# The square between half copies at batch turns, and the passage from attention to the experts with two experts' rows turned together and w1 split one expert ahead

## The chip, the cores and the metric

One core of a Trainium2 chip runs the whole program in one launch. The metric is device time in microseconds (us), the median of several executions. The engines are TensorE (PE, matrix products), ScalarE (ACT), VectorE (DVE), GpSimd (POOL) and SyncE (SP), which issues most DMAs. TensorE's clock has two levels, 2.4 and 1.2 GHz; the profile gives the granted clock as a share of the higher one.

## The reference, cut to what matters

Eight batches of 2496 tokens go through an attention without softmax (z has 64 columns, v and u 256), and the 19968 rows that come out go through a mixture of experts: the gate picks one of eight experts a row, and each expert keeps the 80 rows with the highest gate weight.

```python
scores = scale * np.matmul(z, z.transpose(0, 2, 1))     # scale = 1 / 2496
attn = np.maximum(scores, 0.0) ** 2
x = u * np.matmul(attn, v)
...
logits = x @ w_gate                                     # 8 experts
expert_idx = np.argmax(logits, axis=1)
gate_w = softmax(logits)[row, expert_idx]
...
h = np.maximum(x[tok_idx] @ w1[e], 0.0)                 # w1[e] 256 x 1024, 80 rows
out[tok_idx] = gate_w[tok_idx, None] * (h @ w2[e])      # w2[e] 1024 x 256
```

Rows that no expert keeps stay zero.

## The kernel before, in words

Attention goes batch by batch (`b`), in five chunks of 512 queries (`qc`, the last has 448), and for each chunk over ten pairs of key tiles (`r` counts them). Two accumulators in PSUM (`acc`, one for each half `c` of the 256 columns) collect a chunk; there are two such buffers in all, so the next chunk's first product into one waits until it has been emptied. The scores `s` have one buffer. They are made two steps ahead of their use: PE writes `s`, ACT takes the relu into `a` and squares it there, ACT casts a high part `ah` and DVE subtracts the low part `al`; three products of high and low parts with the split `vt` give the precision of fp32. Scores below the diagonal are not computed again but read back transposed (`blk`); `mirrored` makes `ah` and `al` of them.

At a chunk's last pair `take` copies both accumulators to SBUF (`xf`) on ACT; `chunk_add`, `chunk_x`, `chunk_rest` and `chunk_lo` on DVE make the attention's rows from them, `chunk_logits` and `chunk_sum` the gate's logits. The gate's weights, the ranks of rows within an expert (`blocks`, `count`) and the look-ups of the rows that are likely to be kept (`lookup`, `lookup_rest`, `fetch_two`, `place_two`, `tokens`) stand between the pairs at positions that `two_at` and `finished` write out. A turn from one batch to the next is the step `r` = 9 of chunk 4.

The order on PE, ACT, DVE and POOL is the order in which the code is written (`manual_schedule`); each engine runs its own list and waits at semaphores for the others.

The passage follows the last chunk of batch 7. It finishes the last rows (`chunk_x_last`), their logits and gate, and runs the first products of experts 0 and 1 (`first_products`), with weights that were loaded and split beside the last attention chunks (`LOADS`, `SPLITS`, `kept`). Then `ahead` runs the experts: 512 KB pieces of weights come into five slots, ACT casts their high part and DVE subtracts the low part (`split`), and for each expert PE transposes its rows (`ffn_x`), takes the first product (`ffn1`), transposes the hidden rows (`ffn_h`) and takes the second (`ffn2`); `result` scales by the gate and scatters. The five slots lie where attention had its raw `z`, `v` and weights.

Of the kernel before, what the change touches and what calls it, by code (L numbers as in the profile page):

```python
# [19 lines left out]
P = 128  # L20
# [5 lines left out]
def attn_moe_kernel(ctx, tc, zT, uT, v, wg, w1, w2, out, seq, cap):  # L26
# [51 lines left out]
    zpool = main.enter_context(tc.tile_pool(name="zpool", bufs=2))  # L78
    upool = main.enter_context(tc.tile_pool(name="upool", bufs=1))
# [174 lines left out]
    two_b = [const.tile([P, DC * NS], F32, tag=f"two{i}", name=f"two{i}") for i in range(2)]  # L254
# [121 lines left out]
    def mirrored(b, qc, k):  # L376
# [15 lines left out]
    def scores(b, qc, k, later=False):

        if k // QT < qc:
            return lambda: mirrored(b, qc, k)
# [17 lines left out]
        if later:  # L413
            return lambda: (square(), split(b, qc, k, a, diag, lower, c0, nq))
        square()
        return lambda: split(b, qc, k, a, diag, lower, c0, nq)

    def split(b, qc, k, a, diag, lower, c0, nq):
# [13 lines left out]
        if diag and not lower:  # L432
            quarter_out(b, qc, a)
# [81 lines left out]
    def take(b, qc, c):  # L515
# [4 lines left out]
        nc.scalar.copy(out=x[:, :, c], in_=acc_t[b, qc][c][:, :, :x.shape[-1]])  # L520

    def chunk_add(b, qc):
        x = x_sum[b, qc]
        tt(x[:, 0], x[:, 0], x[:, 1], ALU.add)
# [14 lines left out]
    def chunk_x_last(b, qc, c):  # L539
        x, acc = x_sum[b, qc], acc_t[b, qc][c]  # L540
        for s in (slice(0, 2 * P), slice(2 * P, min(CH, seq - qc * CH))):
            nc.scalar.copy(out=x[:, 1, c, s], in_=acc[:, 1, s])
            tt(x[:, 0, c, s], acc[:, 0, s], x[:, 1, c, s], ALU.add)
            V.scalar_tensor_tensor(out=x[:, 0, c, s], in0=x[:, 0, c, s], scalar=CSQ,
                                   in1=u_t[b, qc][:, c, s], op0=ALU.mult, op1=ALU.mult)

    def chunk_logits_last(b, qc):
# [3 lines left out]
        pl = ps_m.tile([P, 2, CH], F32, tag="m", name=f"pl_{b}_{qc}")[:, 0]  # L551
# [34 lines left out]
    def raw_tile(name):  # L586
        return zpool.tile([P, DC, CH], F32, tag="vraw", name=name, bufs=3)
# [126 lines left out]
    def count(b, k0, n, slot):  # L714

        kr = RB[b] * BPB + k0
        pool, tag = (ps_a, "acc") if b == B - 1 else (ps_m, "m")
        tp = pool.tile([P, 2, CH], F32, tag=tag, name=f"tp_{b}_{k0}")[:, :, :n * E]
# [97 lines left out]
    def first_x():  # L816
        xf = xall[0][:, 0]
        xp = ps_m.tile([P, 2, CH], F32, tag="m", name="xp_first")[:, 0]
        for c in range(DC):
            nc.tensor.transpose(out=xp[:, c * NS:(c + 1) * NS], in_=xf[:NS, c * P:(c + 1) * P],  # L820
                                identity=ident[:NS, :NS])
        x_t[0] = [const.tile([P, DC * NS], F32R, tag=f"two{i}", name=f"x_first{i}") for i in range(2)]
        xh, xl = x_t[0]
        nc.scalar.copy(out=xh, in_=xp[:, :DC * NS])
        tt(xl, xp[:, :DC * NS], xh, ALU.subtract)

    h_first = {}
    x_second = [const.tile([P, DC * NS], F32R, name=f"x_second{i}") for i in range(2)]

    def first_products():  # L830
        one = vpool.tile([P, QT * 2 * D], F32, tag="vt", name="h_first")
        xp = ps_m.tile([P, 2, CH], F32, tag="m", name="xp_second")[:, 0]
        for c in range(DC):
            nc.tensor.transpose(out=xp[:, c * NS:(c + 1) * NS], in_=xall[0][:NS, 1, c * P:(c + 1) * P],
                                identity=ident[:NS, :NS])
        x_t[1] = x_second
        nc.scalar.copy(out=x_t[1][0], in_=xp[:, :DC * NS])
        tt(x_t[1][1], xp[:, :DC * NS], x_t[1][0], ALU.subtract)
        hp = ps_s.tile([P, 2, CH], F32, tag="s", name="hp_first")
        for part in range(2):  # L840
            product1(hp[:, part], 0, 0, part, NS)
        h_first[0] = one[:, :F]
        nc.scalar.activation(out=h_first[0][:NS], in_=hp[:NS].rearrange("p a f -> p (a f)"), func=AF.Relu)
        hp = ps_a.tile([P, 2, CH], F32, tag="acc", name="hp_second")
        for part in range(2):
            product1(hp[:, part], 1, 1, part, NS)
        h_first[1] = vpool.tile([P, QT * 2 * D], F32, tag="vt", name="h_second")[:, :F]
        nc.scalar.activation(out=h_first[1][:NS], in_=hp[:NS].rearrange("p a f -> p (a f)"), func=AF.Relu)
# [13 lines left out]
    def both(f, *es):  # L862
        for e in es:
            f(e)

    two_at = {(2, 2, 3): lookup, (2, 2, 4): lookup_rest,
              (2, 2, 5): lambda: both(fetch_two, 0, 1),
              (2, 2, 9): lambda: (both(place_two, 0, 1), both(fetch_two, 2, 3)),
              (2, 3, 7): lambda: (both(place_two, 2, 3), both(fetch_two, 4, 5)),
              (3, 2, 3): lambda: (both(place_two, 4, 5), both(fetch_two, 6, 7)),  # L870
              (3, 3, 8): lambda: both(place_two, 6, 7),
              (4, 2, 3): tokens,
              (4, 2, 4): lambda: fetch_gates(range(4)), (4, 2, 5): lambda: fetch_gates(range(4, E))}
# [44 lines left out]
    def load_raw(e, which, part, after=None):  # L918
        pool, tag, n = (late["raw"], "wraw", None) if "raw" in late else (zpool, "vraw", 3)
# [69 lines left out]
    SPLITS = dict(zip([(qb, 2), (qb, 4), (qb, 6), (qb, 7), (qz, 2), (qz, 6), (qz, 8), (qz, 9)], early))  # L989
# [21 lines left out]
    def weights_ahead(qc, r):  # L1011
# [11 lines left out]
        if qc == NQ - 1 and r >= NP - 2:  # L1023
            split_hi(*kept[r - NP + 2][0], kept[r - NP + 2][1])
# [21 lines left out]
    def finished(b, qc, r):  # L1046
# [589 lines left out]
```

## Time and profile before

| what | us |
|---|---|
| median of 3 runs | 1327.08 |
| lowest and highest | 1325.53, 1327.59 |
| the profiled execution | 1328.22 |
| its span, first to last instruction | 1326.5 |
| PE, DVE, ACT busy in it | 1300.0, 1063.0, 1017.0 |

The span leaves out the start and the end of the launch, 1.7 us here. The chain of work that ended last runs through PE for 76% of the span. Busy shares are means over stages: attention takes the first 1254 us, the passage some 20, the experts the rest. The mean granted clock of TensorE is 0.994.

### The profile page before, as it was taken

The numbers are of one execution on the slowest core, as the hardware profiler recorded it, in microseconds if no ns is written. First come the engines' busy times: TensorE is split into PE (matmuls) and PEld (weight loads), VectorE is DVE, ScalarE is ACT, GpSimd is POOL, SyncE is SP. The second block draws the span as 40 slices with busy tenths as digits, with TensorE's granted clock in tenths as the row PEclk, the third lists the DMA queues.
The fourth block names the chain that finished last, engine by engine and source line by source line (L and its number), as shares of the span: only waits on it lengthen the run. The fifth ranks groups of instructions, "written<-read, shape, count | busy, mean of one in ns | idle before, by whom it ended". The sixth has DMA issues, their size and how long they took to land.

```text
span 1326.5 us, 31268 instructions
## 1 busy us (share of the span) xinstructions
PE 1300.0 (98%) x13119; PEld 1074.3 (81%) x13119; DVE 1063.0 (80%) x1276; ACT 1017.0 (77%) x1102; POOL 42.8 (3%) x58
## 2 busy tenths in 40 slices
PE   9999999999999999999999999999999999999997
PEld 6888877888877888888888888888888888887786
DVE  8878788678888888787987788877887879867785
ACT  8976688767878688776887778886887768878665
POOL 0000000000001000000003000000000000002011
PEclk9999999999999999999999999999999999999989
DMA  7799768894898949998699958999499985789473
GB/s 215 247 292 265 221 197 242 246 275 158 260 283 248 277 138 280 270 280 244 175 289 280 288 171 236 285 277 269 149 289 277 275 245 161 235 237 269 146 255 119
DMA packets 196132, 317.21 MB, mean 239 GB/s; under 512 B 36192, under 2 KB 119056, under 8 KB 185744
## 3 DMA queue, kind: packets, MB, share of 16 engines
q1 hardware_dynamic: 194704, 312.85, 79.7%
q0 software_dynamic: 1280, 2.30, 0.6%
q8 instruction: 104, 1.70, 0.5%
q14 instruction: 44, 0.36, 0.1%
HBM read 168.77 MB, written 141.21 MB: 234 GB/s over the span
## 4 chain that ended last, share of the span: by engine, by line
PE 76%; DMA 8%; ACT 6%; DVE 4%; issue 3%; SPq 2%; POOL 0%; POOLq 0%; DVEq 0%; ACTq 0%
PE acc L449 61%; PE s L407 10%; DMA blk<-y 3%; DMA y<-x 3%; DVE al L58 2%; ACT a L409 2%; PE pl L612 2%; ACT a L411 1%; PE op L1393 1%; ACT xf L520 1%; PE hp L858 1%; SPq L343 1%; ACT ah L387 1%; DMA zraw<-zT 1%; DMA vraw<-v 1%
## 5 line engine op out<-in xcount | busy, mean ns | idle before, releaser
L449 PE MATMUL acc<-ah,vt 64*128 64x512 f32 (+1 forms) x6240 | 954.4, 383 | 1.3 <-ACT xf L520 1.0
L449 PEld LDWEIGHTS acc<-ah,vt 64*128 64x128 f32 x6240 | 586.6, 184 | 115.6 <-ACT xf L520 8.9
L449 PE MATMUL acc<-al,vt 64*128 64x512 f32 (+1 forms) x3120 | 612.3, 383 | 4.5 <-DVE al L58 4.0
L58 DVE TENSOR_TENSOR al<-a,ah 128x1024 fp32r<-128x1024 f32 (+1 forms) x240 | 270.7, 1128 | 151.1 <-ACT ah L114 147.7
L449 PEld LDWEIGHTS acc<-al,vt 64*128 64x128 f32 x3120 | 300.2, 184 | 66.8 <-DVE al L58 13.0
L409 ACT ACTIVATE a<-s 128x1024 f32<-128x1024 f32 x240 | 229.0, 954 | 148.7 <-PE s L407 127.5
L411 ACT ACTIVATE a<-a 128x1024 f32<-128x1024 f32 x240 | 238.0, 992 | 7.4
L58 DVE TENSOR_TENSOR al<-blk,ah 128x1024 fp32r<-128x1024 f32 x160 | 192.6, 1218 | 51.4 <-ACT ah L387 49.5
L387 ACT CAST ah<-blk 128x1024 fp32r<-128x1024 f32 x160 | 163.9, 1050 | 83.2 <-PE acc L449 75.7
L114 ACT CAST ah<-a 128x1024 fp32r<-128x1024 f32 (+3 forms) x217 | 213.5, 984 | 5.9
L316 DVE STREAM_TRANSPOSE x<-a 128x1024 f32<-128x1024 f32 x160 | 198.1, 1238 | 0.0
L58 DVE TENSOR_TENSOR xf<-xf 128x1024 f32<-128x1024 f32 (+3 forms) x117 | 144.5, 1235 | 0.0
L520 ACT COPY xf<-acc 128x1024 f32<-128x1024 f32 (+1 forms) x78 | 76.8, 996 | 22.5 <-PE acc L449 21.3
L407 PE MATMUL s<-zl,zh 64*128 64x512 f32 x480 | 89.7, 370 | 0.0
L407 PE MATMUL s<-zh,zl 64*128 64x512 f32 x480 | 89.7, 370 | 0.0
L407 PE MATMUL s<-zh,zh 64*128 64x512 f32 x320 | 64.1, 397 | 3.7 <-ACT a L409 3.7
L407 PEld LDWEIGHTS s<-zl,zh 64*128 64x128 f32 x480 | 45.1, 184 | 8.3
L407 PEld LDWEIGHTS s<-zh,zl 64*128 64x128 f32 x480 | 45.2, 185 | 6.8
L147 DVE TENSOR_TENSOR vt<-vraw,vt 128x1024 fp32r<-128x1024 f32 x40 | 48.3, 1207 | 0.0
L528 DVE SCALAR_TENSOR_TENSOR xf<-xf,ut 128x1024 f32<-128x1024 f32 (+1 forms) x39 | 45.8, 1174 | 0.0
L407 PEld LDWEIGHTS s<-zh,zh 64*128 64x128 f32 x320 | 30.1, 184 | 12.2 <-ACT a L409 6.7
L58 DVE TENSOR_TENSOR al<-md,ah 128x512 fp32r<-128x512 f32 x37 | 25.1, 679 | 12.7 <-ACT ah L427 11.2
(198 smaller groups left out, 660.9 us busy)
## 6 DMA issues: line engine op xcount, KB each, us to landing
y<-x SPq DMA_DIRECT2D x80, 1024.0 KB
blk<-y SPq DMA_DIRECT2D x320, 256.0 KB
out<-idle SPq DMA_DIRECT2D x40, 512.0 KB
vraw<-v SPq DMA_DIRECT2D x32, 512.0 KB
ut<-uT SPq DMA_DIRECT2D x32, 512.0 KB
xu<-xf SPq DMA_DIRECT2D x32, 512.0 KB
wraw<-w SPq DMA_DIRECT2D x30, 512.0 KB
yd<-xd SPq DMA_DIRECT2D x37, 256.0 KB
```

What stands on the lines that cost most here:

```text
L58: V.tensor_tensor(out=o, in0=a, in1=b, op=op)
L114: eng.copy(out=o, in_=i)
L147: e1.tensor_tensor(out=vt[:, :, 1], in0=raw, in1=vt[:, :, 0], op=ALU.subtract)
L316: V.transpose(out=x[:, :, :, t:t + 2].rearrange("p n k t s -> p t k n s"), in_=a)
L387: nc.scalar.copy(out=natural(ah), in_=src)
L407: nc.tensor.matmul(s[:, h, c0:c1], zk[hs, t * P:(t + 1) * P], zq[hs], start=n == 0, stop=n == 2)
L409: nc.scalar.activation(out=a[:, :, c0:c1], in_=s[:, :, c0:c1], func=AF.Relu)
L411: nc.scalar.activation(out=a[:, :, c0:c1], in_=a[:, :, c0:c1], func=AF.Square)
L449: nc.tensor.matmul(acc_t[b, qc][c][:, h, :nq], v_t[b, k // QT][hs, k % QT, iv, c * P:(c + 1) * P], x[hs, k % 2, :nq], start=at not in begu ...
L520: nc.scalar.copy(out=x[:, :, c], in_=acc_t[b, qc][c][:, :, :x.shape[-1]])
L528: V.scalar_tensor_tensor(out=x[:, 0], in0=x[:, 0], scalar=CSQ, in1=u_t[b, qc][:, :, :x.shape[-1]], op0=ALU.mult, op1=ALU.mult)
L612: nc.tensor.matmul(to[:, h, t], xb[i % 3][hs, i // 3, t0:t0 + P], wgs[hs, i // 3], start=i == 0, stop=i == 3 * DC - 1)
```

## The change

In attention: at every chunk's last pair the square of the scores that are made ahead stands between the two accumulators' copies (`between`), where it stood before the copies, or, at batch turns, behind them. For the last chunk of a batch ACT copies only one half of an accumulator and DVE adds the other half out of PSUM. The mirrored pair made at the last pair of a chunk is cast in two halves if the next chunk is 2 or 4. The tables of blocks come a chunk later; look-ups, placings and the low parts of `v` stand at other pairs; gates are gathered one expert a pair.

In the passage: the rows of experts 0 and 1 are transposed together, ahead of the last chunk's end; both first products, expert 0's turn, its second product and its scaling stand in the passage, and the remaining splits between them. In `ahead` the loop begins with expert 1's hidden rows, the pieces of w1 come one expert ahead of w2, and the indices of rows (`rows_out`) are copied on POOL. Raw weights and `v` have a pool of their own (`rawpool`), so that the five slots of `ahead` no longer lie over them.

```diff
+    rawpool = main.enter_context(tc.tile_pool(name="rawpool", bufs=3))
...
-    def mirrored(b, qc, k):
+    def mirrored(b, qc, k, part=None):
...
+        if not part:
+            a_t[b, qc, k] = [pair_tile(tag, b, qc, k) for tag in ("ah", "al")]
+        ah, al = a_t[b, qc, k]
+        nc.scalar.copy(out=natural(ah), in_=src[:, rows])
+        tt(natural(al), src[:, rows], natural(ah), ALU.subtract)
...
         if k // QT < qc:
-            return lambda: mirrored(b, qc, k)
+            if turn and qc % 2 == 0:
+                return None, lambda: (mirrored(b, qc, k, 0), mirrored(b, qc, k, 1))
+            return None, lambda: mirrored(b, qc, k)
...
-        nc.scalar.copy(out=x[:, :, c], in_=acc_t[b, qc][c][:, :, :x.shape[-1]])
+        acc = acc_t[b, qc][c][:, :, :x.shape[-1]]
+        if qc < NQ - 1:
+            nc.scalar.copy(out=x[:, :, c], in_=acc)
+        else:
+            nc.scalar.copy(out=x[:, 1, c], in_=acc[:, 1])
+            tt(x[:, 0, c], acc[:, 0], x[:, 1, c], ALU.add)
...
-    two_at = {(2, 2, 3): lookup, (2, 2, 4): lookup_rest,
...
+    two_at = {(2, 3, 7): lookup, (2, 4, 4): lookup_rest,
...
-            elif r == 9 and b <= 2:
-                kr = RB[b - 1] * BPB
-                blocks(ps_m, "m", gp, oh, kr, kr + BPB, wtwo, (b - 1) * BPB)
+        elif qc == 1 and 0 < b <= 2 and r == 2:
+            kr = RB[b - 1] * BPB
+            blocks(ps_m, "m", gp, oh, kr, kr + BPB, wtwo, (b - 1) * BPB)
...
-                attend_pair(b, qc, 2 * p, True, True, lambda c: take(b, qc, c))
+                def between(c):
+                    take(b, qc, c)
+                    if c == 0:
+                        if square:
+                            square()
+                        while turned:
+                            turned.pop()()
+
+                attend_pair(b, qc, 2 * p, True, True, between)
...
+    def first_turns():
+        tp = first["tp"] = ps_s.tile([P, 2, CH], F32, tag="s", name="tp_first")
+        for j in range(FC):
+            to = tp[:, j * 2 // FC, j % (FC // 2) * NS:(j % (FC // 2) + 1) * NS]
+            nc.tensor.transpose(out=to, in_=h_first[0][:NS, j * P:(j + 1) * P], identity=ident[:NS, :NS])
...
+            for x, w in ((hh, w2h), (hh, w2l), (hl, w2h)):
+                nc.tensor.matmul(op[:NS], x[:, i, at], w[:, j], start=n == 0, stop=n == 3 * FC - 1)
+                n += 1
...
-        first_products()
+        first_product(0)
+        p = SPLITS.pop(None)
+        split_w(*p, w_raw.pop(p), V)
+        first_relu(0)
+        first_product(1)
+        split_rest()
         split_rest()
         gate_near(b, 0)
+        first_turns()
         chunk_store(*prev)
         chunk_logits_last(*prev)
+        first_hidden()
+        first_relu(1)
         count(b, 0, BPB - 2, b)
         gate_top(b, NQ - 1, NQ)
         gate_exp(b, NQ - 1)
+        first_second()
         gate_near(b, NQ - 1)
         gate_rows(b, ex_last, gp, nc.gpsimd)
+        first_result()
...
-            pieces = [(e, w, part) for e in range(E) for w in (1, 2) for part in range(2)
-                      if (e, w, part) not in early and (e, w) not in RAW.values()]
+            pieces = [(e, w, part) for i in range(2, E + 1) for e, w in ((i, 1), (i - 1, 2)) for part in range(2)
+                      if e < E and (e, w, part) not in early and (e, w) not in RAW.values()]
...
-                ts(slo_i[e][:NS], nh[0][1][:NS, e:e + 1], 0.0, ALU.add)
+                nc.gpsimd.tensor_scalar(out=slo_i[e][:NS], in0=nh[0][1][:NS, e:e + 1], scalar1=0.0,
+                                        scalar2=None, op0=ALU.add)
```

ScalarE at the first batch turn: `acc_4_0` and `acc_4_1` are the last chunk's accumulators, `a_0_4` and `a_0_6` scores of the next batch. Before:

```order
L409 ACTIVATE a_0_4_2456<-s_0_4_2457 128x1024
L520 COPY xf_4_2477<-acc_4_0_2092 128x2x448
L520 COPY xf_4_2477<-acc_4_1_2093 128x2x448
L411 ACTIVATE a_0_4_2456<-a_0_4_2456 128x1024
L114 CAST ah_0_4_2487<-a_0_4_2456 128x1024
L409 ACTIVATE a_0_6_2495<-s_0_6_2496 128x1024
```

Now:

```order
L415 ACTIVATE a_0_4_2457<-s_0_4_2458 128x1024
L536 COPY xf_4_2478<-acc_4_0_2097 128x448
L417 ACTIVATE a_0_4_2457<-a_0_4_2457 128x1024
L536 COPY xf_4_2478<-acc_4_1_2098 128x448
L115 CAST ah_0_4_2492<-a_0_4_2457 128x1024
L415 ACTIVATE a_0_6_2501<-s_0_6_2502 128x1024
```

The square stands between the copies, and each copy has one half of 448 elements instead of both.

VectorE at the same turn, from the first low part of the next batch on (`xd` is the transposed diagonal, `vt` a split of `v`, `lg` the sum of logits). Before:

```order
L58 TENSOR_TENSOR al_0_0_2424<-a_0_0_2413,ah_0_0_2423 128x1024
L352 STREAM_TRANSPOSE xd_0_2427<-a_0_0_2413 128x2x2x4x32
L619 TENSOR_REDUCE lg_1166<-pl_3_2358 128x32
L147 TENSOR_TENSOR vt_3_2411<-vraw_3_2085,vt_3_2411 128x4x256
L58 TENSOR_TENSOR al_0_4_2488<-a_0_4_2456,ah_0_4_2487 128x1024
L316 STREAM_TRANSPOSE x_1_0_2491<-a_0_4_2456 128x2x4x4x32
```

Now:

```order
L58 TENSOR_TENSOR al_0_0_2429<-a_0_0_2418,ah_0_0_2428 128x1024
L58 TENSOR_TENSOR xf_4_2478<-acc_4_0_2097,xf_4_2478 128x448
L353 STREAM_TRANSPOSE xd_0_2482<-a_0_0_2418 128x2x2x4x32
L58 TENSOR_TENSOR xf_4_2478<-acc_4_1_2098,xf_4_2478 128x448
L58 TENSOR_TENSOR al_0_4_2493<-a_0_4_2457,ah_0_4_2492 128x1024
L317 STREAM_TRANSPOSE x_1_0_2496<-a_0_4_2457 128x2x4x4x32
L638 TENSOR_REDUCE lg_1167<-pl_3_2363 128x32
```

Two additions out of PSUM stand around the transpose `xd`, and the split of `vt` has gone to another place.

TensorE in the passage, from the last product of attention on (`hp` first products, `pl` logits, `op` second products, `xp` and `tp` transposes of rows and hidden rows). Before:

```order
L449 MATMUL acc_4_1_17848<-ah_4_18_18134,vt_4_16024 128x448
L834 MATMUL xp_second<-ident,xall 128x112 x2
L858 MATMUL hp_first<-w1h_43_17523,x_first_17905 112x512
L858 MATMUL hp_second<-w1h_47_17937,x_second_215 112x512
L553 MATMUL pl_4_18276<-idle 128x32
L557 MATMUL pl_4_18276<-wg_sb,xf_4_18194 128x8 x8
L722 MATMUL tp_0_18286<-oh,ones_b 128x64
L1378 MATMUL tp_0_18367<-ident,h_first 128x112 x4
L1378 MATMUL tp_4_18374<-ident,h_first 128x112 x4
L1348 MATMUL xp_18381<-ident,xall 128x112 x2
L1449 MATMUL tp_end<-oh,ones_b 128x8
L1393 MATMUL op_18422<-w2h_45_17680,hTh_18365 112x256
```

Now:

```order
L461 MATMUL acc_4_1_17888<-ah_4_18_18176,vt_4_16060 128x448
L901 MATMUL hp_first_18267<-w1h_43_17561,x_first_17947 112x512
L901 MATMUL hp_first_18284<-w1h_47_17979,x_first_17947 112x512
L869 MATMUL tp_first<-ident,h_first_18282 128x112 x8
L572 MATMUL pl_4_18315<-idle 128x32
L576 MATMUL pl_4_18315<-wg_sb,xf_4_18230 128x8 x8
L743 MATMUL pl_4_18315<-oh,ones_b 128x64
L886 MATMUL op_first<-w2h_45_17718,hT_firsth 112x256
L1409 MATMUL xp_18427<-ident,xall 128x112 x2
L1436 MATMUL tp_0_18442<-ident,h_first_18331 128x112 x4
L1436 MATMUL tp_4_18449<-ident,h_first_18331 128x112 x4
```

Of each run of products the first row stands here. The transposes of expert 1's rows have gone from the head of the passage, and expert 0's turn stands ahead of the logits and its second product right behind the count, where three sets of transposes and the count of the end stood between.

## Rows read from the trace of the kernel before

**Rows 1.** The page's first part: busy time and share of the span.

```profile
PE 1300.0 (98%) x13119; PEld 1074.3 (81%) x13119; DVE 1063.0 (80%) x1276; ACT 1017.0 (77%) x1102; POOL 42.8 (3%) x58
```

**Rows 2.** Waits of PE: line, waited for, us in total, times, longest.

```profile
PE s L407 <- ACT a L409: 4.9, 8, 1.1
PE acc L449 <- DVE al L58: 4.0, 12, 0.5
...
PE wp L884 <- DVE lg L619: 1.3, 2, 0.7
PE acc L449 <- ACT xf L520: 1.0, 2, 0.8
```

**Rows 3.** Timeline at a batch turn: start, us, instruction, idle before it.

```profile
1096.69 1.73 ACT L520 COPY xf<-acc 128x896 f32<-128x896 f32 x2
1098.32 1.06 ACT L411 ACTIVATE a<-a 128x1024 f32<-128x1024 f32 x1
...
1100.36 1.02 ACT L409 ACTIVATE a<-s 128x1024 f32<-128x1024 f32 x1
...
1096.71 0.70 DVE L352 STREAM_TRANSPOSE xd<-a 128x512 f32<-128x512 f32 x1
...
1100.06 0.62 PE L449 MATMUL acc<-ah,vt 64*128 64x512 f32 x4
1100.51 0.39 PE L449 MATMUL acc<-al,vt 64*128 64x512 f32 x2
1101.43 0.50 PE L407 MATMUL s<-zh,zh 64*128 64x512 f32 x2 [0.54 <-ACT a L409]
```

**Rows 4.** Timeline at the beginning of a chunk qc=4.

```profile
1071.26 2.94 ACT L387 CAST ah<-blk 128x1024 fp32r<-128x1024 f32 x3
...
1072.35 2.36 DVE L58 TENSOR_TENSOR al<-blk,ah 128x1024 fp32r<-128x1024 f32 x2 [2.35 <-ACT ah L387]
...
1072.76 0.57 PE L449 MATMUL acc<-ah,vt 64*128 64x448 f32 x4
1073.62 0.47 PE L449 MATMUL acc<-al,vt 64*128 64x448 f32 x2 [0.30 <-DVE al L58]
```

**Rows 5.** Timeline of PE in the passage.

```profile
1253.82 0.41 PE L834 MATMUL xp_second<-ident,xall 112*128 112x112 f32 x2
...
1259.03 0.48 PE L858 MATMUL hp_second<-w1h,x_second 128*112 128x512 f32 x1 [2.03 <-ACT x_second L837]
...
1267.86 1.73 PE L1378 MATMUL tp<-ident,h_first 112*128 112x112 f32 x8 [2.33 <-DVE d_last L58]
...
1270.22 0.54 PE L1393 MATMUL op<-w2h,hTh 128*112 128x256 f32 x1
...
1274.83 0.93 PE L1378 MATMUL tp<-ident,h_second 112*128 112x112 f32 x8
```

**Rows 6.** Busy time by stretch: stretch, length, engines (instructions), PE's granted clock, DMA share, GB/s.

```profile
1264.00:1266.00 2.00, 1.52 (x15) 1.40 (x15) 0.32 (x2) 0.44 (x1) 0.00 (x0) 1.00 1.00 337
...
1268.00:1270.00 2.00, 2.00 (x13) 1.92 (x14) 1.83 (x5) 0.91 (x2) 0.00 (x0) 0.50 0.34 97
...
1280.00:1290.00 10.00, 10.00 (x75) 8.83 (x74) 8.98 (x19) 7.93 (x13) 0.96 (x1) 1.00 0.85 282
1290.00:1300.00 10.00, 10.00 (x70) 8.84 (x69) 9.07 (x15) 9.12 (x13) 1.88 (x2) 1.00 0.82 251
```

**Rows 7.** Timeline of the expert stage: SP, DVE, PE and ACT.

```profile
1256.57 2.44 SPq L925 DMA_DIRECT2D wraw<-w  x5
...
1273.57 2.36 DVE L947 TENSOR_TENSOR w1l<-wraw,w1h 128x1024 fp32r<-128x1024 f32 x2
...
1309.02 0.15 DVE L62 TENSOR_SCALAR idx<-sel 112x1 int32<-112x1 f32 x1
1309.08 1.15 DVE L58 TENSOR_TENSOR hTl<-tp,hTh 128x448 fp32r<-128x448 f32 x2
...
1311.64 0.35 PE L1393 MATMUL op<-w2h,hTh 128*112 128x256 f32 x1
...
1317.98 0.47 ACT L1400 ACTIVATE ob<-op,gates 112x256 f32<-112x256 f32 x1 [2.34 <-PE op L1393]
```

More of the change, by code (lines that the diff above doesn't have):

```diff
@@ L411, in square, with cast @@
             nc.scalar.activation(out=a[:, :, c0:c1], in_=a[:, :, c0:c1], func=AF.Square)
[L413 to L414 removed]
+        def cast():
+            split(b, qc, k, a, diag, lower, c0, nq)
+        if turn:
+            return square, cast
         square()
[L416 removed]
+        return None, cast
     def split(b, qc, k, a, diag, lower, c0, nq):
@@ L540, in chunk_x_last @@
         x, acc = x_sum[b, qc], acc_t[b, qc][c]
[L541 to L545, printed above, removed]
+        s = slice(0, min(CH, seq - qc * CH))
+        nc.scalar.copy(out=x[:, 1, c], in_=acc[:, 1, s])
+        tt(x[:, 0, c], acc[:, 0, s], x[:, 1, c], ALU.add)
+        V.scalar_tensor_tensor(out=x[:, 0, c], in0=x[:, 0, c], scalar=CSQ, in1=u_t[b, qc][:, c, s],
+                               op0=ALU.mult, op1=ALU.mult)
     def chunk_logits_last(b, qc):
@@ L716, in count @@
         kr = RB[b] * BPB + k0
-        pool, tag = (ps_a, "acc") if b == B - 1 else (ps_m, "m")
-        tp = pool.tile([P, 2, CH], F32, tag=tag, name=f"tp_{b}_{k0}")[:, :, :n * E]
+        if b == B - 1:
+            tp = first.pop("count")[:, :, :n * E]
+        else:
+            tp = ps_m.tile([P, 2, CH], F32, tag="m", name=f"tp_{b}_{k0}")[:, :, :n * E]
         rows = [slice(0, P)] if b < 2 or b == B - 1 else HALVES
@@ L816, in first_x @@
     def first_x():
[L817 to L839, printed above, removed]
-        for part in range(2):
[L841 to L848, printed above, removed]
@@ new lines, in first_x @@
+        n = DC * NS
+        xp = ps_m.tile([P, 2, CH], F32, tag="m", name="xp_first")[:, 0, :2 * n]
+        for e in range(2):
+            for c in range(DC):
+                nc.tensor.transpose(out=xp[:, (e * DC + c) * NS:(e * DC + c + 1) * NS],
+                                    in_=xall[0][:NS, e, c * P:(c + 1) * P], identity=ident[:NS, :NS])
+        xh, xl = (const.tile([P, 2 * n], F32R, tag=f"two{i}", name=f"x_first{i}") for i in range(2))
+        nc.scalar.copy(out=xh, in_=xp)
+        tt(xl, xp, xh, ALU.subtract)
@@ new lines, in first_x, with first_product, first_relu @@
+        for e in range(2):
+            x_t[e] = xh[:, e * n:(e + 1) * n], xl[:, e * n:(e + 1) * n]
+    h_first, first = {}, {}
+    def first_product(e):
+        pool, tag = ((ps_s, "s"), (ps_a, "acc"))[e]
+        hp = first[e] = pool.tile([P, 2, CH], F32, tag=tag, name=f"hp_first{e}")
+        for part in range(2):
+            product1(hp[:, part], e, e, part, NS)
+    def first_relu(e):
+        one = vpool.tile([P, QT * 2 * D], F32, tag="vt", name=f"h_first{e}")
+        h_first[e] = one[:, :F]
+        if e == 0:
+            first["out"] = one[:, F:F + D]
+        nc.scalar.activation(out=h_first[e][:NS], in_=first.pop(e)[:NS].rearrange("p a f -> p (a f)"),
+                             func=AF.Relu)
@@ L1051, in finished @@
             rest = 4
+        if qc == NQ - 2 and not at_end:
+            total = 9
         if r == rest:
@@ L1357, in ffn1 @@
             ns = num(i)
-            if not own and i in h_first:
-                h_t[i] = h_first[i]
-                return
             if part == 0:
@@ L1397, in result @@
         def result(i, gg, slo):
-            ns, op = num(i), o_t.pop(i)
-            ob = to.tile([P, D], F32, tag="ob", name=f"ob_{i}{own}")
-            nc.scalar.activation(out=ob[:ns], in_=op[:ns, :D], func=AF.Copy, scale=gg[:ns])
+            ns = num(i)
+            if not own and i == 0:
+                ob = first["out"]
+            else:
+                op = o_t.pop(i)
+                ob = to.tile([P, D], F32, tag="ob", name=f"ob_{i}{own}")
+                nc.scalar.activation(out=ob[:ns], in_=op[:ns, :D], func=AF.Copy, scale=gg[:ns])
             nc.gpsimd.indirect_dma_start(
```

151 lines of the change are left out of this document (84 added, 67 removed).

## The prediction

> **What bounds the kernel now.** I read the shares first. TensorE (PE) is busy for 98% of a span of 1326.5 us [rows 1], so the whole kernel can only win what PE idles (26.5 us, of which some 8.5 lie after its last matmul, 1317.98 [rows 7]) or what it spends at half clock. The view of PE's waits then says who keeps it idle: score matmuls wait for ScalarE's (ACT) relu `a` eight times for 4.9 us, products wait for VectorE's (DVE) `al` twelve times for 4.0 us, and `wp` waits for DVE twice, 1.3 us [rows 2]. The timelines of these places show the queue behind each wait [rows 3, 4]. In the passage the single waits are larger, 2.03 and 2.33 us, and there the granted clock is down to half [rows 5, 6]. In the expert stage PE does not wait, but DVE and ACT are busy for nine tenths [rows 6]; that decides what the stage can give.
>
> **The change, attention.** Times in the rows hold an idle and a slower restart, so I take a gap from start to start and subtract the usual one.
>
> Batch turns (seven). ACT runs two copies of 896 elements a partition from 1096.69 (1.73), then the square and the cast, and only at 1100.36 the relu of the next scores, 1.02 long [rows 3]. PE needs that relu's buffer: its last two `al` matmuls start at 1100.51, the scores at 1101.43, 0.92 later, where two matmuls take 0.23 (four take 0.45, from 1100.06 to 1100.51). Loss 0.69 each. After the change ACT copies one half (two copies, about 0.53 each by the elements, together 0.8 to 0.9 less than now) and DVE adds the other half; the relu ends about 0.85 earlier, at 1100.54 instead of 1101.39. PE would have come at 1100.74, so the wait goes with a margin of 0.2. The price: an accumulator is free only after DVE's add, and the second add stands behind a transpose (0.70). In times of before, the first copy ends 1097.2, its add 1097.85, the transpose 1098.5, the second copy (behind the square, an estimate of 1.1 as of the relu's size) 1098.8, the second add 1099.4, just when PE wants that accumulator. I charge 0.12 a turn and take 7 x 0.57 = 4.0; bounds 0 and 4.8.
>
> Half copies (eight chunks qc=4). PE starts four `ah` matmuls at 1072.76 and `al` at 1073.62, 0.86 later, against 0.40 usual (0.45 x 448/512). ACT casts the first pair 1071.26 to about 1072.3 and DVE's `al` begins at 1072.35 only then, 1.2 long [rows 4]. In halves, DVE starts after half a cast, about 0.5 earlier, less the fixed part of two more instructions: 0.46 each is gone, 3.7 in all. Lower bound half of it, if the fixed parts eat the rest. The eight chunks qc=2 show no wait, so their halves cost nothing on PE; DVE was idle 2.35 before such a copy and hides them.
>
> Tables of blocks: two waits of 0.65 behind a sum in the same PSUM buffer [rows 2]; a quarter chunk later that buffer is free. Gain 1.3. Look-ups: of the twelve waits for `al` the two longest, 0.5 each, stand at the look-ups of batch 2 [rows 2]. The small DVE operations stand now where mirrored pairs are read. Gain 1.0, bounds 0 and 1.4. A turn inside batch 7: 0.8 behind ACT's copies [rows 2], which stand behind a square there. The first copy now comes before the square and the second behind it, so I count 0.4. Placing of experts 4 and 5 moves into a chunk qc=4 of batch 3, where DVE has less room, and the gathers of gates come beside a pair each: I charge 0.6. Sum: 4.0 + 3.7 + 1.3 + 1.0 + 0.4 - 0.6 = 9.8.
>
> **The change, passage and experts.** Before: PE idles 2.03 at 1259.03, because expert 1's rows wait on ACT and DVE behind the last chunk's pieces; then 2.33 at 1267.86 behind the last softmax; and expert 0's second product from 1270.22 runs at half clock [rows 5, 6]. After: both experts' rows are turned together ahead of this, and PE has first products, turns, logits, count and expert 0's second product in one row. From 1253.82 to the end of that second product at 1274.83 PE took 21.0 [rows 5]. The idles go (4.4). At half clock the eight turns took 1.73 instead of 0.93, the second product 4.6 instead of 2.9 (two of them and four turns take 6.3 at full clock, from 1311.64 to 1317.98 [rows 7]), and expert 1's first product an estimated 1.4 more than its 12 x 0.23: together 3.9. Turns and counts of about 1.2 move behind it. What is left, 11.5, puts that end at 1265.3. PE alone would gain about 9. But the expert stage needs the split weights. The chain that chooses rows ends on DVE before the split at 1273.57 [rows 7]. In the new order it still hangs on the logits, on splits that the weights' loads release (asked for at 1256.57 before; at about 1247 now, when nothing else is in the way), and on a count behind the next expert's turn, and I find its end at 1273.1. Behind it stand 20 splits of 512 KB pieces, before and after. From 1273.57 to the last turn's `hTl`, 1309.08 + 1.15 = 1310.23, pass 36.7 us; DVE was busy for 8.98 and 9.07 of each 10 [rows 6], so it had 33.1 us of work. Five copies of indices go to GpSimd (0.15 each), which leaves 32.3. If PE no longer sets the pace, DVE runs through: 1273.1 + 32.3 = 1305.4. Expert 6's second product then starts at about 1305.4 instead of 1311.64, and the rest behind it keeps its 6.3 us [rows 7]. Gain of this stage: 6.2, bounds 4 (ACT, 7.93 and 9.12 of 10 [rows 6], falls out of step with DVE and both lose a tenth of the 32 us, less what the earlier loads give back) and 9 (DVE reaches the stage early enough for PE to bound it).
>
> The early loads cost nothing that I can see: the new pool takes SBUF, not time. `flags`, `flag_all` and `gate_sum` come one expert later, under cover of PE's full stretches [rows 6], and cost nothing while the sums of counts stay ahead of the end.
>
> **The sum.** The profiled execution took 1328.22 us, 1.7 beyond its span and 1.1 above the median. 9.8 + 6.2 = 16.0 off: 1312.2 for such an execution, 1311.1 at the median. A change of 0.2% (2.7 us) is about the least that this kernel's measurement tells from none.
>
> **Rivals.**
> 1. PE bounds the expert stage (chance 0.13). For it: PE showed no wait there and was full in each stretch. Against it: DVE at nine tenths, which cannot shrink. The stage gains 9 and the time is 1308.
> 2. The attention's waits move on (0.15). The margins are 0.2 us at a turn and none for the second accumulator, and each small wait that goes lets PE run into ACT and DVE sooner. Then the turns and half copies give 2 to 3 of 7.7, attention 4 instead of 9.8, and the time is 1317. For it: DVE has no gap between its `al` rows at 1072.35. Against it: DVE sat idle 2.35 right before [rows 4].
> 3. The clock falls in the passage although PE does not idle (0.08). The granted clock was 1.00 at 1264 to 1266, through the narrow logit matmuls, and 0.50 at 1268 to 1270, after an idle of 2.33 [rows 5, 6], so on these rows an idle comes ahead of the fall. If ten transposes and the narrow matmuls bring it down without one, expert 0's second product takes 1.7 longer (4.6 against 2.9, above), and the logits and the next turns 1 to 2 more; DVE's chain hides 1 of it. The stage gains 3.5 and the time is 1314. The Trainium skill (TensorE: Matmul & The Clock Gate, Part 4: PE-mode transpose) says that transposes do not count as busy for the clock in the same way, which would bring this case about; the row at 1268 to 1270, with ten transposes, is at 0.50, but behind an idle, so no row of before tells the two causes apart.
> 4. Slower (0.02): the half clock stays on through the expert stage. PE is full there at 1.00, 10 us in each 10 [rows 6], and at 1.2 GHz each microsecond of that work costs one more. The gain of 16 is used up when 16 us of work run at half beyond what did before; if all from 1274 to 1310 did it would cost some 36 against that 16: about 1347. Against it: the clock stood at 0.50 while expert 0's second product ran and was back at 1.00 by 1280 [rows 6].
> 5. The change does nothing measurable (0.03): both the attention's waits reappear in full and DVE finds itself as late as before, 1327.
>
> My own case holds 0.59: 1311, between 1307.5 and 1314.5 by the bounds (attention 8 to 11, passage 5 to 8). Rivals 1 to 3 lie between 1308 and 1317, so 1305.5 to 1317.5 leaves out the slower side, the unmoved case and the worse half of rival 2, some 2 in 10 with what lies beyond rival 1. Faster: all but rivals 4 and 5, 0.95; same 0.03; slower 0.02.
>
> **What the new profile would show.** Turns: no `s` waiting for ACT's relu, and no `acc` waiting for DVE's add by more than 0.2. Half copies: no wait of `al` at the first pair of chunks qc=4. A batch from turn to turn shorter by about 1.2 us. Passage: PE without an idle over 1 us from the end of attention to expert 0's second product, clock 1.00. Expert stage: DVE without gaps, PE with gaps in front of second products that wait for `hTl`. I am wrong if PE is full in the expert stage (rival 1), if DVE's adds stand in PE's waits (rival 2), or if the clock is 0.5 in the passage (rivals 3 and 4).

## The result, and the profile after

The median fell from 1327.34 us (1325.53 to 1328.23) to 1313.42 us (1311.14 to 1317.60, four executions each), a ratio of 0.990 with a 95% interval of 0.987 to 0.993: 13.9 us faster, where 16.2 were forecast (1311.1, range 1305.5 to 1317.5). The profiled execution took 1315.33 us with a span of 1313.5: 12.9 less than before, against 16.0 in the sum.

The first part of the page, and the waits of PE (line, waited for, us in total, times, longest), of the changed kernel:

```profile
PE 1293.7 (98%) x13119; PEld 1070.5 (81%) x13119; DVE 1064.3 (81%) x1286; ACT 1011.6 (77%) x1115; POOL 52.3 (4%) x66
...
PE acc L461 <- DVE al L58: 3.4, 3, 2.6
...
PE op L1451 <- DVE hTl L58: 1.4, 1, 1.4
...
PE s L413 <- ACT a L415: 1.1, 1, 1.1
```

Beside [rows 2]: seven of the eight waits of `s` are gone (the one left stands at the start, 7.51), `wp` has none, and of the twelve waits for `al` three are left. But one of these is 2.6 long; none was over 0.5 before. It stands in the last chunk of batch 2. The timeline there, DVE, then PE, and the windows of it (stretch, length, PE, PEld, DVE, ACT and POOL busy with their instructions, granted clock, DMA share, GB/s):

```profile
460.56 0.43 DVE L123 CAST zh<-zraw 128x512 fp32r<-128x512 f32 x1 [2.27 <-DMA zraw<-zT]
461.02 0.69 DVE L58 TENSOR_TENSOR zl<-zraw,zh 128x512 fp32r<-128x512 f32 x1
461.63 1.22 DVE L148 TENSOR_TENSOR vt<-vraw,vt 128x1024 fp32r<-128x1024 f32 x1
462.76 0.32 DVE L58 TENSOR_TENSOR fw_two<-fw_two,two 128x160 f32<-128x160 f32 x1
...
465.29 0.16 DVE L58 TENSOR_TENSOR few<-few,f 128x1 f32<-128x1 f32 x1
465.56 1.23 DVE L58 TENSOR_TENSOR al<-blk,ah 128x1024 fp32r<-128x1024 f32 x1
...
463.68 0.59 PE L461 MATMUL acc<-ah,vt 64*128 64x448 f32 x4
466.85 0.74 PE L461 MATMUL acc<-al,vt 64*128 64x448 f32 x2 [2.58 <-DVE al L58]
...
464.00:466.00 2.00, 0.27 (x4) 0.00 (x0) 1.75 (x15) 1.97 (x5) 0.78 (x1) 1.00 0.96 282
466.00:468.00 2.00, 1.15 (x6) 1.07 (x8) 2.00 (x3) 0.79 (x1) 1.29 (x2) 0.60 1.06 376
```

DVE idles 2.27 us for a load of `z` that nobody needs yet, splits `z` and `v` (460.56 to 462.76), then runs the look-ups (462.76 to 465.5), and only then makes the `al` that PE waits for. Without the look-ups that `al` could have begun at 462.76 and ended some 0.3 before PE came for it (466.85 less 2.58). The wait costs 2.58, and after it the granted clock is down to 1.2 GHz for a while (0.60 in that window), by an estimate from the windows some 1.7 more. So attention ended at 1245.1 instead of 1253.8: 8.7 gained, and about 4.3 given back on the way.

A batch turn and the beginning of a chunk qc=4 after (ACT, then DVE):

```profile
1088.92 0.53 ACT L536 COPY xf<-acc 128x448 f32<-128x448 f32 x1
1089.35 1.06 ACT L417 ACTIVATE a<-a 128x1024 f32<-128x1024 f32 x1
1090.32 0.52 ACT L536 COPY xf<-acc 128x448 f32<-128x448 f32 x1
...
1091.67 1.04 ACT L415 ACTIVATE a<-s 128x1024 f32<-128x1024 f32 x1
...
1090.87 0.62 DVE L58 TENSOR_TENSOR xf<-acc,xf 128x448 f32<-128x448 f32 x1
...
1064.05 3.04 ACT L391 CAST ah<-blk 128x512 fp32r<-128x512 f32 x4
...
1064.70 1.30 DVE L58 TENSOR_TENSOR al<-blk,ah 128x512 fp32r<-128x512 f32 x2 [1.93 <-ACT ah L391]
```

From the first copy to the next relu's start ACT now takes 2.75 us, where it took 3.67 [rows 3]; DVE's `al` of the first mirrored pair starts 0.65 after ACT's cast, where it started 1.09 after [rows 4].

What PE gains there is read from start to start. The first mirrored pair of a chunk qc=2 before, the end of that of a chunk qc=4 before (its start is in [rows 4]), then the same two after, and the products ahead of the scores at a batch turn after:

```profile
1011.74 0.61 PE L449 MATMUL acc<-ah,vt 64*128 64x512 f32 x4
1012.43 0.50 PE L449 MATMUL acc<-al,vt 64*128 64x512 f32 x2
1012.76 0.62 PE L449 MATMUL acc<-ah,vt 64*128 64x512 f32 x4
...
1073.93 0.57 PE L449 MATMUL acc<-ah,vt 64*128 64x448 f32 x4
...
1004.89 0.62 PE L461 MATMUL acc<-ah,vt 64*128 64x512 f32 x4
1005.58 0.62 PE L461 MATMUL acc<-ah,vt 64*128 64x512 f32 x4
...
1065.54 0.57 PE L461 MATMUL acc<-ah,vt 64*128 64x448 f32 x4
1066.16 0.57 PE L461 MATMUL acc<-ah,vt 64*128 64x448 f32 x4
...
1092.35 0.62 PE L461 MATMUL acc<-ah,vt 64*128 64x512 f32 x4
1093.04 0.39 PE L413 MATMUL s<-zh,zh 64*128 64x512 f32 x2
```

At qc=4 the six products took 1.17 and take 0.62, in all eight batches. At qc=2 they took 1.02 and take 0.69; there the waits of PE showed nothing, and yet six of the eight batches lost this third of a microsecond (batches 1 and 2 did not). The turn took 1.37 from the four products to the scores (1100.06 to 1101.43 [rows 3]) and takes 0.69, seven times. In all that is 6.4 for the half copies and 4.8 for the turns.

The passage and the expert stage after: timeline of PE, windows, then DVE, PE and ACT.

```profile
1250.76 0.93 PE L869 MATMUL tp_first<-ident,h_first 112*128 112x112 f32 x8
...
1253.40 0.35 PE L886 MATMUL op_first<-w2h,hT_firsth 128*112 128x256 f32 x1
...
1250.00:1252.00 2.00, 2.00 (x18) 1.74 (x17) 1.82 (x2) 1.37 (x3) 0.00 (x0) 1.00 0.36 136
...
1276.00:1286.00 10.00, 10.00 (x77) 9.24 (x77) 9.93 (x15) 9.34 (x13) 2.75 (x3) 1.00 0.95 344
...
1264.36 2.36 DVE L989 TENSOR_TENSOR w2l<-wraw,w2h 128x1024 fp32r<-128x1024 f32 x2
...
1295.56 1.15 DVE L58 TENSOR_TENSOR hTl<-tp,hTh 128x448 fp32r<-128x448 f32 x2
...
1269.58 0.37 PE L1451 MATMUL op<-w2h,hTl 128*112 128x256 f32 x1 [1.37 <-DVE hTl L58]
...
1302.90 0.47 ACT L1462 ACTIVATE ob<-op,gates 112x256 f32<-112x256 f32 x1 [2.34 <-PE op L1451]
```

Eight transposes and the logits ran at 1.00; expert 0's second product takes 2.9 us at full clock; DVE is busy for 9.93 of 10. From the first product to the last `ob` passed 57.8 us (1245.12 to 1302.90) against 64.0 before (1254.00 to 1317.98): 6.2 gained, and 0.2 more because the transposes of expert 1's rows no longer stand ahead of the first product (1253.82 [rows 5]). What follows the last `ob` is longer, though: 10.6 us to the end of the span, where it was 8.5. So 8.7 + 6.2 + 0.2 - 2.1 = 13.0.

### The profile page after: what moved, and what is told of

Same layout as the page of the kernel before. It is cut to its first block, busy times and chain, and to the rows that moved or that the text cites. A ratio compares the mean times of both kernels' runs of the same rounds, so it can differ in the third digit from the quotient of the medians.

```text
span 1313.5 us, 31282 instructions
## 1 busy us (share of the span) xinstructions
PE 1293.7 (98%) x13119; PEld 1070.5 (81%) x13119; DVE 1064.3 (81%) x1286; ACT 1011.6 (77%) x1115; POOL 52.3 (4%) x66
## 4 chain that ended last, share of the span: by engine, by line
PE 87%; DVE 4%; DMA 3%; ACT 3%; issue 2%; SPq 0%; POOL 0%; POOLq 0%; DVEq 0%; ACTq 0%
PE acc L461 73%; PE s L413 11%; PE pl L631 2%; DMA blk<-y 1%; DVE al L58 1%; DMA out<-idle 1%; DVE w1l L989 1%; ACT a L415 1%; DMA zraw<-zT 1%; ACT a L417 1%; DVE w2l L989 1%; PE hp_first L901 0%; DVE xf L58 0%; ACT ah L115 0%; DMA wraw<-w 0%
## 5 line engine op out<-in xcount | busy, mean ns | idle before, releaser
L58 DVE TENSOR_TENSOR al<-blk,ah 128x1024 fp32r<-128x1024 f32 (+1 forms) x176 | 194.4, 1123 | 46.8 <-ACT ah L391 46.6
L391 ACT CAST ah<-blk 128x1024 fp32r<-128x1024 f32 (+1 forms) x176 | 164.8, 973 | 75.4 <-PE acc L461 66.7
L58 DVE TENSOR_TENSOR xf<-xf 128x1024 f32<-128x1024 f32 (+2 forms) x110 | 137.3, 1249 | 0.0
L534 ACT COPY xf<-acc 128x1024 f32<-128x1024 f32 x64 | 64.9, 1016 | 22.3 <-PE acc L461 21.7
L413 PE MATMUL s<-zh,zh 64*128 64x512 f32 x320 | 63.5, 394 | 0.0
L631 PEld LDWEIGHTS <-xf 64*128 64x128 bf16 x1872 | 26.1, 93 | 9.9 <-issue 9.9
```

The lines of the kernel that those rows point to most:

```text
L58: V.tensor_tensor(out=o, in0=a, in1=b, op=op)
L391: nc.scalar.copy(out=natural(ah), in_=src[:, rows])
L413: nc.tensor.matmul(s[:, h, c0:c1], zk[hs, t * P:(t + 1) * P], zq[hs], start=n == 0, stop=n == 2)
L534: nc.scalar.copy(out=x[:, :, c], in_=acc)
L631: nc.tensor.matmul(to[:, h, t], xb[i % 3][hs, i // 3, t0:t0 + P], wgs[hs, i // 3], start=i == 0, stop=i == 3 * DC - 1)
```

## The experiments

Times are compared with the kernel before in the same series, whose median there was 1329.54 (the first four kernels), 1330.21 (the next four) and 1331.38 (the last four).

| kernel | median | ratio to before, 95% | first product to last ob | last ob to end |
|---|---|---|---|---|
| again | 1314.31 | 0.988 (0.986 to 0.989) | 57.3 | 10.4 |
| rest_early | 1314.02 | 0.988 (0.986 to 0.989) | 57.8 | 10.7 |
| no_turn | 1323.12 | 0.996 (0.994 to 0.997) | 57.7 | 10.7 |
| no_half | 1318.98 | 0.992 (0.990 to 0.993) | 57.5 | 10.6 |
| both_early | 1310.56 | 0.986 (0.984 to 0.988) | 57.3 | 10.3 |
| rows_dve | 1313.79 | 0.987 (0.986 to 0.989) | 58.1 | 11.0 |
| dve_more | 1318.36 | 0.991 (0.990 to 0.993) | 63.5 | 10.3 |
| passage_only | 1326.69 | 0.997 (0.997 to 0.998) | 58.2 | 10.3 |
| attention_only | 1317.50 | 0.990 (0.988 to 0.991) | 63.5 | 8.6 |
| z_late | 1312.45 | 0.986 (0.985 to 0.988) | 57.2 | 10.9 |
| whole_copies | 1321.76 | 0.993 (0.992 to 0.994) | 57.3 | 10.4 |
| pool_splits | 1318.61 | 0.990 (0.988 to 0.991) | 61.8 | 10.4 |

**again**, no edit. 

> The changed kernel once more, for its spread (1311.1 to 1317.6 so far). Theory: the spread is the wait at 466.85, where DVE's look_up_rest stands behind a load of z that comes late: an execution near 1311 shows that wait under 1 us and no half clock behind it, one near 1316 shows 2.5 or more and a stretch at 0.5. Rival: the spread lies at the end, behind the last scatter; then the wait at 466 is the same 2.6 in a profile of 1311.

The profiled execution, 1315.15, has the same wait (2.65 at 465.56), one of 0.50 at 620.65 that the first profile lacks, and 10.4 at the end. The runs go from 1310.6 to 1316.5, and no profile fell near 1311: where the spread lies was not shown here.

**rest_early.**

```diff
-(2, 4, 4): lookup_rest
+(2, 4, 3): lookup_rest
```

> lookup_rest one pair earlier, at (2, 4, 3), where DVE sat idle 2.3 us for the load of z. Theory (the 2.6 us of small operations behind that idle made the wait of 2.58 and the stretch at half clock): the wait goes, batch 2 is shorter by 4.3 (2.58 and some 1.7 of half clock), the median is 1309 to 1311 and the spread under 2. Rival (the load of z is late and would stop PE wherever the look-ups stand): a wait of 2 us or more stays near 465, the median stays at 1313 or more.

Both are half right. The wait at 464 is 0.29, but the time is that of `again`: 1.96 us (and a stretch at half clock) now stand at the same place of batch 3. The timeline of DVE and PE there:

```profile
614.77 0.43 DVE L123 CAST zh<-zraw 128x512 fp32r<-128x512 f32 x1 [3.25 <-DMA zraw<-zT]
...
616.98 0.47 DVE L803 TENSOR_SCALAR_CACHE_REDUCE lw_two<-two,rin 112x256 bf16<-112x256 bf16 x1
...
617.90 1.22 DVE L58 TENSOR_TENSOR al<-blk,ah 128x1024 fp32r<-128x1024 f32 x1
...
619.17 0.47 PE L461 MATMUL acc<-al,vt 64*128 64x448 f32 x2 [1.96 <-DVE al L58]
```

In the first profile of the changed kernel DVE idled 0.81 for that load, here 3.25, and the placing of experts 4 and 5 (616.98 to 617.9) stands behind it. The placing is 0.92 of the 1.96; the rest is the load itself and the splits of `z` and `v` behind it. A load that arrives when it likes, in front of a queue in order, with small work of the change behind it: that was my next theory.

**both_early**, rest_early and one more look-up moved:

```diff
-(3, 4, 4): lambda: (both(place_two, 4, 5), ...
+(3, 4, 3): lambda: (both(place_two, 4, 5), ...
```

> rest_early, and the placing of experts 4 and 5 in batch 3 one pair earlier as well, (3, 4, 3), where DVE idled 3.25 us for the late load of z in rest_early. Theory (small DVE operations behind a late z load are what stops PE in a chunk qc=4): the waits of 1.96 at 619 and of 0.29 at 464 are gone or under 0.4, no stretch at half clock before the end, 3 to 4 faster than rest_early (1314.0 by the runs of before at 1329.5), so about 1310.5, or 0.9855 of before. Rival (each wait that goes turns up at the next late z load, as from 466 to 619): a wait of about 2 at a chunk qc=4 of another batch, and 1313 to 1315.

Waits of PE in it:

```profile
PE acc L461 <- DVE al L58: 1.1, 3, 0.6
```

1310.56, 19.7 below before; attention ends at 1241.65. Of the three waits for `al` two are 0.23 and 0.30, and the third, 0.56, stands in the last chunk of batch 7. In this execution the rival did not come; but DVE idled only 0.58 for this load in batch 3, and **pool_splits** below, with the same attention, shows a later one.

**z_late**, the changed kernel with DVE's split of `z` one pair later:

```diff
-keys_in[NQ - 1] = [(NQ - 2, 1, 4), (NQ - 1, 4, 7)]
+keys_in[NQ - 1] = [(NQ - 2, 1, 5), (NQ - 1, 4, 7)]
```

> The changed kernel with look-ups and placing where the change put them, but DVE's split of z, which waits for a load, one pair later in the last chunk, behind the low part that PE wants. Theory (DVE stands idle at the late load and all behind it is late): the waits at 466 and 620 go or fall under 0.6, 3 faster than the changed kernel, about 0.986 of before, as both_early. Rival (the 2.6 us of look-ups alone make the wait): a wait of 1.5 to 2.5 stays at 466, and 0.988 of before.

No wait at 466 or 620 is left, though the look-ups and the placing are where the change put them; attention ends at 1240.85. In its profile this load of batch 3 was there when DVE came to it (614.68), so how this order bears a late one is not shown. Its time is that of both_early within the intervals; both intervals overlap with those of again and rest_early, so the medians alone do not tell a cure from a load that came in time.

**no_turn** (on rest_early).

```diff
-if qc < NQ - 1:
-    nc.scalar.copy(out=x[:, :, c], in_=acc)
-else:
-    nc.scalar.copy(out=x[:, 1, c], in_=acc[:, 1])
-    tt(x[:, 0, c], acc[:, 0], x[:, 1, c], ALU.add)
+nc.scalar.copy(out=x[:, :, c], in_=acc)
...
-if c == 0:
+if c == int(qc == NQ - 1):
     if square:
         square()
```

> rest_early with the batch turns as before (ACT copies both halves, the square behind both copies, DVE adds in SBUF). Theory (the turns gave 0.57 to 0.69 each, seven times): 4.0 to 4.8 slower than rest_early, and waits of s for ACT's relu of about 0.5 at seven turns. Rival (waits only move on): within 1.5 of rest_early.

9.1 slower than rest_early, twice what the theory said. PE's timeline at one turn and 12 us behind it:

```profile
169.06 0.50 PE L413 MATMUL s<-zh,zh 64*128 64x512 f32 x2 [0.54 <-ACT a L415]
...
181.13 0.50 PE L461 MATMUL acc<-al,vt 64*128 64x512 f32 x2 [0.44 <-DVE al L58]
```

Both come seven times. The first is the wait of [rows 3]. The second was not there before: the sum of halves on DVE now stands right ahead of a split of `vt` that the change moved into the new batch (1107.85, 1.05, and 1108.83, 1.21, then `al` at 1109.95). So DVE's two short additions at the turn also pay for the place of that split. Batch 6, from its first product to that of batch 7, takes 154.48 here and 152.97 in rest_early.

**whole_copies** (on both_early): the first of no_turn's two hunks alone; the square stays between the copies. 

> both_early with the square still between the copies at batch turns, but ACT copying both halves and DVE adding in SBUF as before. Theory (the turn gains by the half that ACT does not copy, and by the sum that DVE no longer makes later, not by the order): waits of s for ACT's relu of about 0.5 at seven turns and of al of 0.4 some 12 us behind each, 8 slower than both_early, as no_turn. Rival (the order of square and copies gains): under 4 slower.

About 10 slower than both_early by the ratios. The wait of `s` is 0.22 instead of 0.54, the one of `al` 0.43 as in no_turn. That looks like 0.3 a turn for the order of the square, but batch 6 takes 154.49 here, 154.48 in no_turn and 152.92 in both_early: at the end of a batch nothing is left of it, and the halves make the difference. Whether the order counts beside half copies, as the change has it, no run shows. This profile has waits of 0.45 and 1.11 at late loads besides (466.80 and 622.39).

**no_half** (on rest_early).

```diff
-if turn and qc % 2 == 0:
+if False:
     return None, lambda: (mirrored(b, qc, k, 0), mirrored(b, qc, k, 1))
```

> rest_early with the mirrored pair at a chunk's turn cast whole. Theory (0.46 each at eight chunks qc=4): 3.7 slower than rest_early, waits of al of 0.3 at the first pair of the eight chunks qc=4 and none at chunks qc=2. Rival: the halves give half of it or nothing, since the shorter wait is taken up by the next product: under 1.5 slower.

5.0 slower. Waits of 0.30 at the first pair of chunks qc=4 are back (1072.38 in one, and 0.30 or 0.31 in all but one of the eight), and none at chunks qc=2. The waits are not the whole of it, though: without the halves the first mirrored pair's six products take 1.01 to 1.04 at qc=2 in all eight batches, against 0.68 or 0.69 in rest_early, and 1.17 to 1.19 at qc=4 in seven, against 0.61. So the halves give some 7. The medians' 5.0 also holds the late loads of both kernels, which differ from one execution to the next: 0.86 and 1.69 here, 1.96 and a stretch at half clock in rest_early.

**dve_more** (on both_early).

```diff
 split_w(*p, raw, V)
+if p[1:] == (1, 1):
+    hi, lo = wt[p[0], 1]
+    tt(lo[:, 1:], raw, hi[:, 1:], ALU.subtract)
```

> both_early with DVE's subtract of the second half of w1 done twice for experts 3 to 7: five operations of 1.14 in a row with others, 5.7 more on DVE, the same results. Theory (DVE bounds the expert stage): 4.5 to 5.7 slower. Rival (PE or the loads bound it): under 2 slower.

The stage is 6.2 longer for 5.7 more of DVE, the median 7.8. A wait of 3.91 for `hTl` with a stretch at half clock behind it stands in the stage; the 0.5 beyond DVE's work may be that, which was not separated. DVE bounds the expert stage.

**pool_splits** (on both_early).

```diff
-split_w(*p, raw, V)
+split_w(*p, raw, nc.gpsimd if p in ((3, 2, 1), (4, 2, 1), (5, 2, 1)) else V)
```

> both_early with three of the low parts of w2 (second halves for experts 3 to 5) subtracted on GpSimd, 3.4 less on DVE in the expert stage. Theory (DVE bounds the stage): 1.5 to 3.4 faster than both_early, 1307.5 to 1309. Rival (GpSimd's subtract is several times slower, holds up its scatters or DVE): no gain or slower by up to 3.

The stage is 4.5 longer, the median some 5 by the ratios, where the theory had a gain. GpSimd's third subtract and the one of DVE beside it:

```profile
1288.56 2.40 POOL L989 TENSOR_TENSOR w2l<-wraw,w2h 128x1024 fp32r<-128x1024 f32 x1 [0.74 <-ACT w2h L979]
...
1288.64 3.39 DVE L989 TENSOR_TENSOR w2l<-wraw,w2h 128x1024 fp32r<-128x1024 f32 x1
```

DVE's takes 3.39 instead of 1.22: it loses 2.17 of the 2.40 that GpSimd runs. The work moves off DVE and its time does not.

The same profile answers what both_early left open. In batch 3 the placing is over (611.84) before DVE comes to the load, and nothing small stands behind it. DVE, PE and a window there:

```profile
616.74 0.43 DVE L123 CAST zh<-zraw 128x512 fp32r<-128x512 f32 x1 [3.68 <-DMA zraw<-zT]
...
618.95 1.22 DVE L58 TENSOR_TENSOR al<-blk,ah 128x1024 fp32r<-128x1024 f32 x1
...
620.22 0.47 PE L461 MATMUL acc<-al,vt 64*128 64x448 f32 x2 [2.40 <-DVE al L58]
...
620.00:622.00 2.00, 1.78 (x12) 1.63 (x14) 2.00 (x3) 1.90 (x3) 0.00 (x0) 0.72 0.89 215
```

So a load that is late enough stops PE without any look-up behind it, and the batch is 4.0 longer than in both_early. To move the small work takes off its own share of the wait (all of it at 466 in the changed kernel, 0.92 of 1.96 in rest_early) and leaves the load's.

**rows_dve** (on both_early): the copies of row indices on DVE as before, `ts(slo_i[e][:NS], nh[0][1][:NS, e:e + 1], 0.0, ALU.add)`. 

> both_early with the copies of row indices back on DVE. In the changed kernel the span ends 10.6 us after the last ob starts, 8.5 before. Theory (GpSimd's copies stand ahead of the last scatters and make them late): the end is 8.5 again, and DVE has 0.5 more of work in the expert stage, so 1 to 2 faster than both_early. Rival (the longer end has to do with the last scatter's landing, not with what GpSimd does before): the end stays at 10.3 to 10.7, the time within 1 of both_early.

The end stays long, at 11.0; the theory falls. The median is 3.2 slower, more than either theory had, though the intervals overlap; in the profile: 0.8 of it in the expert stage, 0.7 at the end, the rest in attention (0.71 at a late load, a later start), which the edit does not touch.

**attention_only** and **passage_only**: the kernel before with one of the two parts, attention_only with the look-ups as in both_early. 

> The kernel before with only the edits of attention, the look-ups and the placing one pair earlier as in both_early. Theory (the two parts add up): attention 11 to 12 shorter, the passage and the expert stage as before (64.0 from the first product to the last ob), and 8.5 from the last ob to the end, since the longer end belongs to the new passage: 11 to 12 faster than before. Rival (the end's 2 us are a matter of the execution, not of the passage's code): 10.2 or more from the last ob to the end.

> The kernel before with only the edits of the passage and of the experts' order. Theory: from the end of attention to the last ob 6.2 to 6.4 less than before, the end behind it 2 longer, attention as before: 4 to 6 faster than before. Rival (the passage gains only because attention ends with DVE less behind): under 3 faster.

attention_only is 13.9 faster, more than the 11 to 12 expected, with the two idles of the passage (2.02 and 1.98) and the half clock behind them. It ends 8.6 behind the last `ob`, passage_only 10.3: the longer end belongs to the new passage's code. passage_only has its stage 5.8 shorter, and is 3.5 faster. In its profile attention is 3.1 longer than before, at one place (ACT idle 4.68 up to 729.33 in batch 4), which I cannot put down to an edit; GpSimd gathers the gates beside it, as it does in the kernel before without such a loss. The two parts, 13.9 and 3.5, make 17.4 of both_early's 19.7; the rest stays open with that place.

## Why the prediction was right, and where a step was off

The direction and the range held. The likeliest case did too (1307.5 to 1314.5), but of its two sums one came out by luck: in attention 9.8 were forecast and 8.7 measured because two terms, 3.5 too small, nearly make up for a third that missed a loss of 4.3.

- **Passage and experts**, 6.2 forecast, 6.2 measured, by the steps given. I put the end of the rows' choice at 1273.1; it is 1264.36, which is 1273.1 in times of before with attention's 8.7 added. I put the last `hTl` but those of expert 7 at 1305.4; it is 1296.71, again 1305.4. DVE sets the pace (dve_more), so rival 1, the 9 us of PE alone, did not come.
- **Batch turns**, 4.0 forecast, 4.8 measured against the kernel before. All seven waits are gone without the 0.12 that I charged, and no wait for DVE's adds took their place. Undone, they cost 9.1: I had set them against the kernel before and not against the new places of `vt`'s splits.
- **Half copies**, 3.7 forecast, 6.4 measured. "The eight chunks qc=2 show no wait, so their halves cost nothing on PE" put a gain of 2.0 at nothing: the loss of 0.33 there showed in the starts of the products and not in the waits. (The idle of 2.35 that I gave for these chunks is one of qc=4; at 1011.15 DVE idled 1.43.) At qc=4 each gave 0.55 instead of 0.46. **Tables of blocks**: both waits of `wp` gone, as forecast.
- **Look-ups**, the step that failed: "The small DVE operations stand now where mirrored pairs are read. Gain 1.0". The waits of batch 2 did go, but 2.58 and some 1.7 of half clock came at the new place, and the charge of 0.6 did not cover it. I priced the operations by DVE's mean room and not by what stands ahead of them in its queue. Without that wait attention gives 12.2 (both_early), against my 9.8 with its charges. The gathers of gates, also in that charge, may cost too: the last chunk of batch 4, where they stand now, takes 28.56 in both_early and that of batch 5 27.01, while in the first profile of the changed kernel both take 27.30. What makes it so was not shown. The row that would have told lay in the trace of before, at the same place of the next batch; with nothing small behind the splits PE waited 0.31 there:

```profile
621.21 0.43 DVE L122 CAST zh<-zraw 128x512 fp32r<-128x512 f32 x1 [2.72 <-DMA zraw<-zT]
```

- **The end** was left out: 2.1 us from the new passage's code, which no step of mine had.
- **Rival 2**, that waits move on, is the nearest to what happened in the changed kernel, at one place and not at the turns; in rest_early and pool_splits it happened at the same place of batch 3. **Rival 3** did not come: the window with eight transposes and the first logits is at 1.00. The rule of the Trainium skill (TensorE: Matmul & The Clock Gate, Part 4: PE-mode transpose) on transposes is not borne out here as a fall of the clock: in this passage, with products ahead of and behind them, it stayed up. The falls ahead of the end of these runs all came after idles, such as 2.58 at 466 in the changed kernel, 1.96 at 619 in rest_early and 3.91 in dve_more.

## What to carry to other kernels

Small work that is moved onto an engine with an in-order queue is priced by what stands right ahead of it there: a place behind an operation that waits for a load is as full as the load is late, however idle the engine is on the mean. Moving the work away saves no more than its own length; a load that comes later still stops the queue by itself. A wait of two microseconds on TensorE is dearer than it reads: the clock fell behind the 1.96 of rest_early, and not behind the 1.69 of no_half. And an edit that frees an engine at one place can be what pays for another edit of the same change, so undo them one at a time before taking their gains from the kernel before. A loss that is short shows in the starts of the products, against those of an undisturbed chunk, and not in the list of waits.

## What the runs showed of the hardware that I had not expected

GpSimd's elementwise work beside DVE's subtract of two SBUF operands takes DVE's time: in pool_splits 1.22 becomes 3.39 beside 2.40 on GpSimd, and two in a row take 4.57 instead of 2.35 beside one of 2.65 (1273.95 and 1274.79). The Trainium skill (GPSIMD Engine Reference, 8. Key points) says that GpSimd shares its SBUF interfaces with VectorE, with contention for DVE instructions that have two SBUF inputs; this trace agrees, nearly one for one. GpSimd's own tiny copies of indices may suffer as well: in the changed kernel one takes 0.27 to 1.04 beside DVE's splits (1.04 at 1264.62), two take 0.39 at 1297.29 with none.

The last scatters' landing. With the new passage it took longer, by the view of DMA issues over the last 12 us (tiles, engine, operation, count, median us from issue to landing) of before and of the changed kernel:

```profile
out<-ob,idx POOLq DMA_INDIRECT x2, 2.6
```

```profile
out<-ob,idx POOLq DMA_INDIRECT x2, 3.6
```

It is 2.6 again in attention_only and 4.1 in passage_only. The last scatter also starts later, 1.62 after the start of the last `ob` against 0.92. What in the code makes it so was not settled. Moving the index copies back (rows_dve) brought the landing to 2.8 and not the end: there the last scatter starts 3.23 after the start of the last `ob`.
